# Loading the weights and x in groups between layer-norm transposes, and pacing q attention against the GLU, in a two-layer transformer kernel on one Trainium2 core

## The chip, the cores and the metric

The kernel runs on one core of one Trainium2 chip. A core has a matrix engine (TensorE, PE in the profile), a vector engine (VectorE, DVE), a scalar engine (ScalarE, ACT), a general engine (GpSimd, POOL) and a small engine that mostly issues transfers (SyncE, SP). Each has its own stream of instructions and works through it in order; they wait for each other on semaphores. Transfers between the main memory and the on-chip memory (SBUF) are issued by an instruction of SP or ACT and are then carried out by 16 DMA engines. Matrix products land in PSUM, which has eight banks here.

The metric is the device time of one execution in microseconds (us); lower is better. Three runs of the kernel before took 1256.72, 1257.25 and 1257.52 us, median 1257.25.

## The reference

x has 2048 tokens of width 576. Two kinds of layer alternate, twice each, every one with a layer norm in front and a residual sum behind:

```python
x = x + A(layernorm(x)); x = x + B(layernorm(x))
x = x + A(layernorm(x)); x = x + B(layernorm(x))

# A: linear attention, 32 heads of width 18
q, k, v = split(x @ wqkv)
phi(t)  = concat(softmax(t @ w_phi), softmax(-(t @ w_phi)))   # per head, 18 -> 36
kv = phi(k)^T @ v          # summed over all tokens
z  = sum of phi(k) over all tokens
o  = (phi(q) @ kv) / (phi(q) . z + 1e-6)
A  = o @ wo

# B: gated linear unit, width 4608, no activation function
B  = ((x @ w_gate) * (x @ w_up)) @ w_down
```

All inputs are bf16. kv and z need phi(k) of every token before the first token's q attention can be finished. That is a barrier in each layer.

## The kernel before

**Tiles.** A *state* is 128 tokens; there are 16. A *block* is two states, 256 tokens; there are 8. x stays in SBUF (`x_sb`) from beginning to end. Gate and up weights (`Wg`, `Wu`, `Wr`) stay there as well; the down weight is read again for each block, in 18 chunks of two 128-row tiles each, through a ring of four slots (`wdr`).

**Stages.** In the order of the work:

1. *Loads* (`t_load`, line 619). x, w_phi, the raw q and k weights, Wv, Wo, then Wr, Wg and Wu, 10.6 MB of them in ten loads. All are issued on ACT's queue.
2. *Fusing* (`t_fuse`, line 671, `t_fuse2`, line 696). w_phi is the same for every token, so the kernel multiplies it into the q and k weights once: PE transposes a raw weight (L688), ACT copies it out (`WT`, L691), PE multiplies it with the block-diagonal w_phi (L709), DVE copies the result to `Wk` or `Wq` (L716). The q weights follow when two states of k attention are through.
3. *Layer norm* of one block (`t_ln`, line 725). DVE computes statistics (L734, L739), ACT the reciprocal root (L746 to L750), POOL normalises each state (L755), ACT copies a tail (L760), and SP issues one transposing transfer per state (L764), which brings `xln` into `xT`, with the features on the partitions. Three pairs of `xln` buffers are in turn.
4. *k attention* of one state (`t_ain`, line 873). PE projects (`proj`, L778), `softmax_front` (line 782) computes both softmaxes over ACT, DVE and POOL (max and min on DVE, L793 and L798; differences on POOL, L803, and DVE, L811; exponentials on ACT, L818 and L820; sums on DVE, L825; the division by the sums as a product on POOL, L839). `t_v` (line 842) projects v (L857 is its copy). PE adds phi(k)^T v to PSUM (L867).
5. *Barrier* (`t_barrier`, line 919). The sums over all 16 states are masked into `BD`.
6. *q attention* of one state (`t_aout`, line 948). The same `softmax_front`, then transposes (L964), the product with `BD` (L981), the division (L993 to L1006), a transpose (L1017), the product with Wo (L778 again) and the sum into x (L1030).
7. *GLU* of one block (`t_bmain`, line 1083, `t_down`, line 1122). First the *gate phase*: 648 matmuls of gate and up (L1070), which take six PSUM banks, copied and multiplied into `hT` (L1113, L1115). Then the *down phase*: 36 tiles times two states, each a matmul of 512 columns (L1137) and one of 64 (L1140). `t_bepi` (line 1150) adds the result to x (L1158) and signals `("x2", L, b)`: layer L, block b.

Layer 1 of A runs for all tokens first. The A part of layer 2 up to its barrier is woven into the GLU of layer 1: when a block is through (`after`, line 1215), its layer norm, k attention and `t_kv` are started.

**What sets the order.** The program is written by a planner (`Sched`, line 246). Each piece of work above is a generator, a *thread* with a priority, that yields lists of instructions for an engine, transfers, requests for buffers and PSUM banks, `wait` and `sig`. The planner keeps its own clock: a duration for each instruction, and for each transfer a start on its queue, a speed and a latency (lines 428 to 439). It takes again and again the instruction list that could start first on that clock, with the higher priority first in a tie, and appends it to its engine's stream. `wait` and `sig` only act in the planner, on the order of the streams. On the chip there are just the semaphores that the data need: a reader waits for its writer, a writer for the readers before it. `record_dma` (line 133) does this for transfers: a transfer waits on its issuing engine's stream, and what stands behind it in that stream waits too.

While a gate phase is planned, the GLU thread holds a lock, and no other thread gets a PSUM bank (line 284). So attention's matmuls stand in the down windows between the gate phases. Before a gate phase of block b the GLU thread waits for its policy (`pol1`, line 1238, `pol2`, line 1246): the q attention of block b+1 must be planned, and in layer 1, from b = 2 on, the k attention of layer 2 for block b-2.

`t_q` (line 1178) starts q attention: for each block in turn it waits until `xT` is there and, from the second block on, for the barrier, starts both states, and waits for the second state of the block before. It does not look at the GLU. Here are the lines:

```python
for b in range(NB):
    yield ("wait", ("xT", L, b))
    if b >= s.early // 2:
        yield ("wait", ("BD", L))
    for j in range(2):
        yield ("go", s.t_aout(L, 2 * b + j), ...)
```

The down-weight thread (`t_wd`, line 1038) and the GLU thread are started once all ten gate and up loads are planned (`wloaded`). In the kernel before this is at once, and the first four chunks are issued at the very start.

Of the kernel before, what the change touches and what calls it, by code (L numbers as in the profile page):

```python
# [17 lines left out]
class Tracker:  # L18
    def __init__(self):
        self.ops = {e: [] for e in ENGINES}  # L20
        self.count = {e: 0 for e in ENGINES}
        self.know = {e: {} for e in ENGINES}
        self.snap = {}
        self.fin = {}
        self.lastw = {}
        self.readers = {}
        self.lastacc = {}
        self.dma_groups = []
        self.pend_w = {}
        self.pend_r = {}  # L30
        self.stats = {"ops": 0, "waits": 0, "multiwait": 0, "pe_multiwait": 0}
# [214 lines left out]
class Sched:  # L246
# [74 lines left out]
    def run(self):  # L321
        tr = self.tr
        while True:
            progressed = False
            again = True
            while again:
                again = False
                for th in list(self.threads):
                    while th.req is not None and th.req[0] not in ("ops", "dma", "acq", "acqn"):
                        r = th.req  # L330
# [52 lines left out]
            for th in self.threads:  # L383
                r = th.req
# [21 lines left out]
            r = th.req  # L406
            if r[0] == "ops":
                eng = r[1]
                t = est
                first = True  # L410
                t_beg = t
                for o in r[2]:
                    deps = tr.deps_for(eng, o.reads, o.writes, o.excl, True, o.order)
                    if not first:
                        t = max(t, tr.ready_time(deps))
                    if eng == "pe" and o.mode != self.pe_mode:
                        self.pe_mode = o.mode
                        if not first:
                            t += self.pe_switch
                    first = False  # L420
                    fin = t + o.dur
                    tr.record(eng, o.emit, o.reads, o.writes, o.excl, fin, deps)
                    self.busy[eng] += o.dur
                    t = fin
                if self.log is not None:
                    self.log.append((th.name, eng, t_beg, t, len(r[2]), self.free_at[eng]))
                self.free_at[eng] = t
            else:
                _, group, emit, reads, writes, nbytes, dram_write = r[:7]
                immediate = r[7] if len(r) > 7 else False  # L430
                issue = est
                queue = r[9] if len(r) > 9 else "sp"
                start = max(issue, self.dma_free[queue])
                xfer = nbytes / self.dma_bw
                self.dma_free[queue] = start + xfer
                sp_time = r[8] if len(r) > 8 else 60.0
                fin = max(start + xfer + self.dma_lat, issue + 2.1 * sp_time)
                tr.record_dma(group, emit, reads, writes, fin, queue, dram_write, immediate)
                self.free_at[queue] = issue + sp_time
# [37 lines left out]
class K:  # L477
    def __init__(self, nc, A_x, A_wqkv, A_w_phi, A_wo, B_w_gate, B_w_up, B_w_down, out):
        self.nc = nc
        self.A_x, self.A_wqkv, self.A_w_phi, self.A_wo = A_x, A_wqkv, A_w_phi, A_wo  # L480
        self.wg, self.wu, self.wd, self.out = B_w_gate, B_w_up, B_w_down, out
        self.NPS, self.NSM, self.NVX, self.NET, self.NXP, self.NWD, self.NG, self.NO = 2, 4, 2, 3, 2, 4, 2, 1
        self.early = 2
        self.qlead = 3
        self.bias = {10: 300.0}
        self.tr = Tracker()
        self.sc = Sched(self.tr)
        self.stack = ExitStack()
# [130 lines left out]
    def t_load(self):  # L619
        s, tr = self, self.tr  # L620
        xv = s.A_x[0].rearrange("(t p) d -> p t d", p=128)
        wqkv = s.A_wqkv

        def grp(name, items, ev):
            g = tr.dma_group(name)
            for emit, writes, nbytes in items:
                yield ("dma", g, emit, (), writes, nbytes, False, False, 60.0, "act")
            yield ("dmaclose", g)
            yield ("sig", ev)

        def xload(j):
            return grp("x%d" % j, [((lambda e: e.dma_start(s.x_sb[:, 4 * j:4 * j + 4, :], xv[:, 4 * j:4 * j + 4, :])),
                                    [("x", t, c_) for t in range(4 * j, 4 * j + 4) for c_ in range(2)], 128 * 4 * D * 2)], ("ld", "x", j))
# [8 lines left out]
        items = []  # L642
        for t in range(NT):
            h0 = T0[t] // DH
            items.append(((lambda e, t=t, h0=h0: e.dma_start(s.wst[:, t, :], s.A_w_phi[h0:h0 + HT].rearrange("j d f -> (j d) f"))),
                          [("wst",)], TW * DH * 2))
        yield from grp("wphi", items, ("ld", "wphi"))
        for kt in range(5):
            yield from rawload("k", kt)

        def w5(W, src, key, name):
            return grp(name, [
                ((lambda e: e.dma_start(W[:, 0:4, :], src[0:512].rearrange("(k p) n -> p k n", p=128))), [(key,)], 512 * D * 2),
                ((lambda e: e.dma_start(W[0:64, 4, :], src[512:576])), [(key, 0)], 64 * D * 2)], ("ld", name))

        yield from w5(s.Wv, wqkv[:, 2 * D:3 * D], "Wv", "wv")
        for j in range(1, 4):
            yield from xload(j)
        for kt in range(5):
            yield from rawload("q", kt)  # L660
        yield from w5(s.Wo, s.A_wo, "Wo", "wo")
        wgv = s.wg[0:512, :].rearrange("(k p) n -> p k n", p=128)
        wuv = s.wu[0:512, :].rearrange("(k p) n -> p k n", p=128)
        items = [((lambda e: e.dma_start(s.Wr[0:64, :], s.wg[512:576, :])), [("Wr",)], 64 * FF * 2),
                 ((lambda e: e.dma_start(s.Wr[64:128, :], s.wu[512:576, :])), [("Wr",)], 64 * FF * 2)]
        for k in range(4):
            items.append(((lambda e, k=k: e.dma_start(s.Wg[:, k, :], wgv[:, k, :])), [("Wg",)], 128 * FF * 2))
            items.append(((lambda e, k=k: e.dma_start(s.Wu[:, k, :], wuv[:, k, :])), [("Wu",)], 128 * FF * 2))
        yield from grp("wgu", items, "wloaded")

    def t_fuse(self, which):
        s = self
# [505 lines left out]
    def t_q(self, L):  # L1178
        s = self

        def pair_done(b):
            yield ("wait", ("x1", L, 2 * b))
            yield ("wait", ("x1", L, 2 * b + 1))
            yield ("go", s.t_ln(b, ("xTB", L, b)), 8, "lnB%d_%d" % (L, b))

        yield ("wait", ("ain", L, NS - s.qlead))
        for b in range(NB):
            yield ("wait", ("xT", L, b))
            if b >= s.early // 2:
                yield ("wait", ("BD", L))  # L1190
            for j in range(2):
                yield ("go", s.t_aout(L, 2 * b + j), 7 + (NS - 2 * b - j) / 100.0, "aout%d_%d" % (L, 2 * b + j))
            yield ("go", pair_done(b), 8, "pd%d_%d" % (L, b))
            if b >= 1:
                yield ("wait", ("x1", L, 2 * b - 1))

    def t_layer1(self):
        s = self
        gots = yield ("acqn", ["pb"], 3)
        s.kvb = [g_[1] for g_ in gots]  # L1200
        yield ("wait", "init")
# [109 lines left out]
```

## Time and profile before

| | value |
|---|---|
| median of three runs | 1257.25 us |
| the profiled execution's own time | 1257.18 us |
| its span in the profile | 1255.4 us |
| mean granted TensorE clock | 0.985 of full speed |
| PE busy | 1125.3 us (90%) |
| DVE, ACT, POOL busy | 591.9, 438.0, 272.8 us |
| read from HBM | 100.59 MB |
| transfers of ACT's queue (q10) | 15.66 MB |
| transfers of SP's queue (q1) | 97.81 MB |

The span is the time from the first to the last instruction of the trace; the difference to the execution's time, 1.8 us, lies around it. Busy PE time is modelled, and a matmul that follows close upon another overlaps with it, so a PE that is busy for 100% of a stretch is not one at its peak. The profile's views used below are: the chain of work that ended last (each piece with its start, its length and what it was), the timeline (start, length, engine, line, operation, tiles, count, and the idle time before it with what ended it), the stretches (for each stretch its length, then the busy time and count of PE, PE's weight loads, DVE, ACT and POOL, the granted clock, the share of the DMA engines and GB/s; with a line given, of that line's instructions alone), and the list of transfer issues. L1070 and the like are lines of the kernel.

### The profile page before, as it was taken

To read this page: it belongs to the slowest core of one execution; us is meant where nothing else is said; L and a number is where in the kernel's file an instruction comes from. 1 tells how busy PE (TensorE), PEld (TensorE's weight loads), DVE (VectorE), ACT (ScalarE), POOL (GpSimd) and SP (SyncE) were. 2 spreads that over 40 slices of the span, in tenths; PEclk is the share of its full clock that TensorE was granted. 3 is DMA by queue.
4 is the path that set the end of the run, shared out by engine and by line. 5 is a ranking of instruction groups with operands and counts; after the bars stand their busy time and mean duration, and the time that the engine had idled before them with its cause. 6 is when DMAs were issued, how large, how long until landed. Compare 5 with 4: busy or idle time off the path is not lost.

```text
span 1255.4 us, 33464 instructions
## 1 busy us (share of the span) xinstructions
PE 1125.3 (90%) x15104; PEld 853.9 (68%) x15172; DVE 591.9 (47%) x1243; ACT 438.0 (35%) x976; POOL 272.8 (22%) x271
## 2 busy tenths in 40 slices
PE   1377689999999999999999759999999999999998
PEld 1155477787786867677777448778685858677684
DVE  3188775848653434343434475674832313122131
ACT  2167544536441314141413344554521212121120
POOL 1268731514311011111111342240500000000000
PEclk9989899999999999999999889999999999999999
DMA  9820011514406061515151401240616060523414
GB/s 293 281 38 12 1 22 36 158 13 110 104 14 179 15 168 32 152 31 153 39 144 50 133 1 23 78 126 10 165 41 182 11 180 21 162 69 113 124 59 142
DMA packets 130315, 115.61 MB, mean 92 GB/s; under 512 B 48892, under 2 KB 129020, under 8 KB 129020
## 3 DMA queue, kind: packets, MB, share of 16 engines
q1 hardware_dynamic: 123520, 97.81, 29.3%
q10 hardware_dynamic: 6652, 15.66, 3.6%
q8 instruction: 119, 1.95, 0.6%
q14 instruction: 24, 0.20, 0.0%
HBM read 100.59 MB, written 2.36 MB: 82 GB/s over the span
## 4 chain that ended last, share of the span: by engine, by line
PE 74%; DMA 13%; DVE 5%; ACT 3%; POOL 2%; ACTq 1%; issue 1%; SPq 0%; DVEq 0%
PE ps L1070 45%; PE ps L1137 12%; DMA wdr<-in_B_w_down_dram 11%; PE ps L778 10%; DMA xT<-xln 3%; PE ps L1140 2%; POOL dd L839 2%; PE ps L964 1%; PE ps L981 1%; PE ps L867 1%; PE ps L1017 1%; DVE o L1006 1%; DVE ss L825 1%; DVE mxmn L793 1%; DVE mxmn L798 1%
## 5 line engine op out<-in xcount | busy, mean ns | idle before, releaser
L1070 PE MATMUL ps<-xT,Wg 64*128 64x256 bf16 x4608 | 568.0, 269 | 1.7 <-DMA xT<-xln 1.7
L1070 PE MATMUL ps<-xT,Wu 64*128 64x256 bf16 x4608 | 568.5, 269 | 0.9 <-DVE x_sb L1158 0.7
L1070 PEld LDWEIGHTS ps<-xT,Wg 64*128 64x128 bf16 x4608 | 429.5, 94 | 32.5 <-issue 2.9
L1070 PEld LDWEIGHTS ps<-xT,Wu 64*128 64x128 bf16 x4608 | 431.7, 94 | 28.7 <-DVE x_sb L1158 1.8
L1115 DVE TENSOR_TENSOR hT<-ps,gsb 128x512 bf16<-128x512 f32 x288 | 199.1, 691 | 341.7 <-ACT gsb L1113 341.3
L1113 ACT CAST gsb<-ps 128x512 bf16<-128x512 f32 x288 | 168.5, 585 | 543.9 <-PE ps L1070 543.3
L1137 PE MATMUL ps<-wdr,hT 128*128 128x512 bf16 x1084 | 293.6, 381 | 20.5 <-DMA wdr<-in_B_w_down_dram 19.7
L1140 PE MATMUL ps<-wdr,hT 128*128 128x64 bf16 x1152 | 221.9, 193 | 5.2 <-DMA wdr<-in_B_w_down_dram 1.2
L1137 PEld LDWEIGHTS ps<-wdr,hT 128*128 128x128 bf16 x1152 | 112.5, 98 | 161.3 <-DMA wdr<-in_B_w_down_dram 45.0
L839 POOL TENSOR_TENSOR dd<-dd,ss 128x576 bf16<-128x576 bf16 x128 | 145.7, 1163 | 112.1 <-ACT ss L833 112.1
L1070 PE MATMUL ps<-xT,Wr 64*128 64x256 bf16 x1152 | 167.3, 269 | 0.0
L803 POOL TENSOR_TENSOR dd<-psb,mxmn 128x576 bf16<-128x576 bf16 x64 | 74.2, 1163 | 324.8 <-DVE mxmn L793 324.8
L1140 PEld LDWEIGHTS ps<-wdr,hT 128*128 128x128 bf16 x1152 | 112.9, 98 | 0.9
L755 POOL TENSOR_SCALAR xln<-x_sb,nmean,rstd 128x576 bf16<-128x576 bf16 x64 | 51.9, 821 | 240.1 <-ACT rstd L750 213.9
L1158 DVE TENSOR_TENSOR x_sb<-ps,x_sb 128x512 bf16<-128x512 f32 x32 | 21.9, 685 | 164.3 <-PE ps L1140 164.3
L825 DVE TENSOR_REDUCE ss<-dd 128x64 f32<-128x1152 bf16 x64 | 85.2, 1341 | 19.7 <-ACT dd L820 19.5
L778 PE MATMUL ps<-Wv,xT 128*128 128x378 bf16 (+1 forms) x320 | 54.5, 306 | 26.1 <-issue 17.6
L793 DVE TENSOR_REDUCE mxmn<-psb 128x32 f32<-128x576 bf16 x64 | 47.6, 744 | 54.6 <-ACT psb L790 54.6
L1070 PEld LDWEIGHTS ps<-xT,Wr 64*128 64x128 bf16 x1152 | 65.3, 94 | 6.8
L790 ACT CAST psb<-ps 128x288 bf16<-128x288 f32 x128 | 50.3, 398 | 41.0 <-PE ps L778 38.7
L778 PE MATMUL ps<-Wk,xT 128*128 128x288 bf16 x320 | 50.6, 300 | 9.7 <-DMA xT<-xln 7.0
L778 PEld LDWEIGHTS ps<-Wv,xT 128*128 128x128 bf16 x320 | 29.9, 103 | 39.8 <-issue 25.7
(67 smaller groups left out, 930.7 us busy)
## 6 DMA issues: line engine op xcount, KB each, us to landing
wdr<-in_B_w_down_dram SPq DMA_DIRECT2D x288, 288.0 KB, 3.3
Wg<-in_B_w_gate_dram ACTq DMA_DIRECT2D x4, 1152.0 KB, 22.4
Wu<-in_B_w_up_dram ACTq DMA_DIRECT2D x4, 1152.0 KB, 24.8
x_sb<-in_A_x_dram ACTq DMA_DIRECT2D x4, 576.0 KB, 7.4
out_dram<-x_sb SPq DMA_DIRECT2D x8, 288.0 KB, 2.9
Wraw<-in_A_wqkv_dram ACTq DMA_DIRECT2D x8, 144.0 KB, 6.2
xT<-xln SPq DMA_TRANSPOSE x64, 2.9
Wv<-in_A_wqkv_dram ACTq DMA_DIRECT2D x1, 576.0 KB, 6.0
```

Source lines behind the costliest of these rows:

```text
L755: ops.append(Op(800, (lambda e, j=j: e.tensor_scalar(xln[:, sl[j], 0:576], x_sb[:, ss[j], :], nm[:, sl[j]:sl[j] + 1], rstd[:, sl[j]:sl[j] ...
L778: ops.append(Op(d_pe(n), (lambda e, lhsT=lhsT, rhs=rhs, k=k: e.matmul(s.ps[:, bank, 0:n], lhsT, rhs, start=(k == 0), stop=(k == 4))), read ...
L790: yield ("ops", "act", [Op(d_actc(288), (lambda e, h=h, bank=bank: e.copy(psb[:, pz, 288 * h:288 * h + 288], s.ps[:, bank, 0:288])), reads ...
L793: ops = [Op(680, (lambda e: e.tensor_reduce(mxmn[:, pz, 0, :], p3, AX.X, ALU.max)), reads=[("psb", pz, 0), ("psb", pz, 1)], writes=[("mx", ...
L803: yield ("ops", "pool", [Op(1170, (lambda e: e.tensor_tensor(d1, p3, mxb, ALU.subtract)), reads=[("psb", pz, 0), ("psb", pz, 1), ("mx", pz ...
L825: Op(1320, (lambda e: e.tensor_reduce(ss[:, sm, :].rearrange("p (b g) -> p b g", b=2), e4, AX.X, ALU.add)), reads=s.ddk(sm, 0) + s.ddk(sm, ...
L839: yield ("ops", "pool", [Op(1150, (lambda e, ev=ev, rb=rb: e.tensor_tensor(ev, ev, rb, ALU.mult)), reads=s.ddk(sm, br) + [("ss", sm)], wri ...
L1070: out.append(Op(54.3, (lambda e, bank=bank, cs=cs, lhsT=lhsT, rhs=rhs, st=st, sp=sp: e.matmul(ps[:, bank, cs], lhsT, rhs, start=st, stop=s ...
L1113: yield ("ops", "act", [Op(540, (lambda e, g=g, gb=gb: e.copy(gsb[:, g, :], ps[:, gb, :])), reads=[("gu", gb)], writes=[("gsb", g)], excl= ...
L1115: yield ("ops", "dve", [Op(625, (lambda e, g=g, ub=ub, p=p: e.tensor_tensor(hT[:, p, :], ps[:, ub, :], gsb[:, g, :], ALU.mult)), reads=[(" ...
L1137: ops.append(Op(d_pe(512), (lambda e, lhsT=lhsT, bank=bank, slot=slot, fi=fi, f=f: e.matmul(ps[:, bank, 0:512], lhsT, s.wdr[:, slot, fi, 0 ...
L1140: ops.append(Op(d_pe(64) + 3, (lambda e, lhsT=lhsT, sl=sl, slot=slot, fi=fi, f=f: e.matmul(ps[:, Z, 64 * sl:64 * sl + 64], lhsT, s.wdr[:, ...
```

## The change

Three things change.

*The queue and the order of the loads.* Every load of `t_load` goes to SP's queue instead of ACT's. x is loaded block by block (eight loads) instead of four loads of two blocks. w_phi comes in two loads instead of five. x of block 1 is planned behind the raw k weights, x of block 2 behind Wv. x of block b, from 3 on, is planned when the transposes of block b-3 of the first layer norm are; raw q goes behind x of block 5, Wo behind x of block 6. The ten gate and up loads are planned in groups: three when the transposes of block 5 are planned, three with block 6, four with block 7. `wloaded` comes at the end of them.

*The planner's time for an issue.* A transfer without a time of its own now occupies its queue for 480 ns on the planner's clock instead of 60. That concerns the loads and the down-weight chunks; the transposes keep their 1250.

*The pace of q attention.* In layer 1, block b's q attention, from b = 4 on, is started only when block b-4 is through the GLU; in layer 2, from b = 3 on, when block b-3 is.

```diff
-                sp_time = r[8] if len(r) > 8 else 60.0
+                sp_time = r[8] if len(r) > 8 else 480.0
...
+        self.pace = (4, 3)
...
-                yield ("dma", g, emit, (), writes, nbytes, False, False, 60.0, "act")
+                yield ("dma", g, emit, (), writes, nbytes, False)
...
-        def xload(j):
-            return grp("x%d" % j, [((lambda e: e.dma_start(s.x_sb[:, 4 * j:4 * j + 4, :], xv[:, 4 * j:4 * j + 4, :])),
+        def xload(b):
+            return grp("x%d" % b, [((lambda e: e.dma_start(s.x_sb[:, 2 * b:2 * b + 2, :], xv[:, 2 * b:2 * b + 2, :])),
...
+        items = [((lambda e: e.dma_start(s.wst[:, 0:4, :], s.A_w_phi[0:4 * HT].rearrange("(t j) d f -> (j d) t f", j=HT))), [("wst",)], TW * DH * 8),
+                 ((lambda e: e.dma_start(s.wst[:, 4, :], s.A_w_phi[H - HT:H].rearrange("j d f -> (j d) f"))), [("wst",)], TW * DH * 2)]
         yield from grp("wphi", items, ("ld", "wphi"))
         for kt in range(5):
             yield from rawload("k", kt)
+        yield from xload(1)
...
         yield from w5(s.Wv, wqkv[:, 2 * D:3 * D], "Wv", "wv")
-        for j in range(1, 4):
-            yield from xload(j)
-        for kt in range(5):
-            yield from rawload("q", kt)
-        yield from w5(s.Wo, s.A_wo, "Wo", "wo")
+        yield from xload(2)
+        for b in range(3, NB):
+            yield ("wait", ("xT", 1, b - 3))
+            yield from xload(b)
+            if b == 5:
+                for kt in range(5):
+                    yield from rawload("q", kt)
+            if b == 6:
+                yield from w5(s.Wo, s.A_wo, "Wo", "wo")
...
-        yield from grp("wgu", items, "wloaded")
+        g = tr.dma_group("wgu")
+        for i, (emit, writes, nbytes) in enumerate(items):
+            if i % 3 == 0 and 5 + i // 3 < NB:
+                yield ("wait", ("xT", 1, 5 + i // 3))
+            yield ("dma", g, emit, (), writes, nbytes, False)
+        yield ("dmaclose", g)
+        yield ("sig", "wloaded")
...
             yield ("wait", ("xT", L, b))
+            if b >= s.pace[L - 1]:
+                yield ("wait", ("x2", L, b - s.pace[L - 1]))
...
-            yield ("wait", ("ld", "x", b // 2))
+            yield ("wait", ("ld", "x", b))
```

More of the change, by code (lines that the diff above doesn't have):

```diff
@@ L626, in grp @@
             for emit, writes, nbytes in items:
-                yield ("dma", g, emit, (), writes, nbytes, False, False, 60.0, "act")
+                yield ("dma", g, emit, (), writes, nbytes, False)
             yield ("dmaclose", g)
             yield ("sig", ev)
-        def xload(j):
-            return grp("x%d" % j, [((lambda e: e.dma_start(s.x_sb[:, 4 * j:4 * j + 4, :], xv[:, 4 * j:4 * j + 4, :])),
-                                    [("x", t, c_) for t in range(4 * j, 4 * j + 4) for c_ in range(2)], 128 * 4 * D * 2)], ("ld", "x", j))
+        def xload(b):
+            return grp("x%d" % b, [((lambda e: e.dma_start(s.x_sb[:, 2 * b:2 * b + 2, :], xv[:, 2 * b:2 * b + 2, :])),
+                                    [("x", t, c_) for t in range(2 * b, 2 * b + 2) for c_ in range(2)], 128 * 2 * D * 2)], ("ld", "x", b))
         def rawload(which, kt):
@@ L641, in t_load @@
         yield from xload(0)
[L642 to L646, printed above, removed]
+        items = [((lambda e: e.dma_start(s.wst[:, 0:4, :], s.A_w_phi[0:4 * HT].rearrange("(t j) d f -> (j d) t f", j=HT))), [("wst",)], TW * DH * 8),
+                 ((lambda e: e.dma_start(s.wst[:, 4, :], s.A_w_phi[H - HT:H].rearrange("j d f -> (j d) f"))), [("wst",)], TW * DH * 2)]
         yield from grp("wphi", items, ("ld", "wphi"))
```

## The prediction

> **What bounds the kernel now.** I read first the chain of work that ended last, in order of time, because shares of busy time mix stages with different limits. Three of its pieces frame the stage ahead of the first GLU block (start us, length us, what):
>
> ```profile
> 25.81 26.80 DMA xT<-xln
> 52.75 5.18 PE ps L778 x20
> ...
> 171.23 35.54 PE ps L1070 x648
> ```
>
> Nothing but a layer-norm transpose is on the chain for 26.8 us, and the first gate block starts at 171.23 us. The timeline of the first 66 us tells why (start, length, engine, line, tile, count, idle time before):
>
> ```profile
> 5.74 1.54 DVE L734 BATCH_NORM_STATS2 st<-x_sb 128x6 f32<-128x288 bf16 x4 [4.41 <-DMA x_sb<-in_A_x_dram]
> ...
> 20.15 0.45 ACTq L668 DMA_DIRECT2D Wu<-in_B_w_up_dram  x1
> 20.64 1.29 ACT L691 COPY WT<-ps 126x640 bf16<-126x640 bf16 x2 [6.25 <-issue]
> ...
> 29.97 0.34 DVE L716 CAST Wk<-ps 64x198 bf16<-64x198 f32 x1
> ...
> 66.22 4.52 POOL L839 TENSOR_TENSOR dd<-dd,ss 128x576 bf16<-128x576 bf16 x4 [3.10 <-ACT ss L833]
> ```
>
> x is there at 5.7 us, but ACT issues loads until 20.6 us and only then takes up the fusing of Wk (L691) and its part of the layer norm. Then the transposes stand beside the bulk loads. Their size and speed: the page's list of DMA issues (KB each, us to landing) and the stretch from 20 to 40 us (last columns: DMA share 1.03, 342 GB/s):
>
> ```profile
> Wg<-in_B_w_gate_dram ACTq DMA_DIRECT2D x4, 1152.0 KB, 22.4
> wdr<-in_B_w_down_dram SPq DMA_DIRECT2D x288, 288.0 KB, 3.3
> 20.00:40.00 20.00, 4.69 (x40) 4.06 (x40) 9.20 (x30) 5.14 (x16) 3.23 (x4) 1.00 1.03 342
> ```
>
> From 66 us on, POOL carries the k attention: two states need 8.5 us (116.86 to 125.39), of which it idles 1.76:
>
> ```profile
> 116.86 4.52 POOL L839 TENSOR_TENSOR dd<-dd,ss 128x576 bf16<-128x576 bf16 x4 [1.76 <-ACT ss L833]
> 121.34 2.29 POOL L803 TENSOR_TENSOR dd<-psb,mxmn 128x576 bf16<-128x576 bf16 x2
> 125.39 4.52 POOL L839 TENSOR_TENSOR dd<-dd,ss 128x576 bf16<-128x576 bf16 x4 [1.76 <-ACT ss L833]
> ```
>
> Behind 171 us PE is the bound. Between two gate phases lies a down phase; only there can attention get PSUM banks (the gate thread holds the lock). I asked for the stretches of these down windows. Layer 1, windows behind blocks 0, 1 and 3, with the sum over windows 0 to 4; then layer 2, windows 0, 1, 5 and the sum over 0 to 5:
>
> ```profile
> 206.77:249.86 43.09, 42.15 (x420) 29.66 (x427) 35.66 (x96) 26.30 (x59) 20.63 (x20) 1.00 0.49 134
> 284.31:329.07 44.76, 43.73 (x429) 30.81 (x437) 36.99 (x95) 25.73 (x61) 21.42 (x20) 1.00 0.51 133
> ...
> 430.20:455.91 25.71, 24.40 (x202) 13.93 (x208) 10.26 (x18) 7.19 (x17) 6.89 (x6) 1.00 0.61 178
> ...
> sum 171.98, PE 163.84 PEld 105.92 DVE 107.85 ACT 76.47 POOL 64.29; mean PE 32.77 PEld 21.18 DVE 21.57 ACT 15.29 POOL 12.86
> ```
>
> ```profile
> 793.96:837.04 43.08, 42.12 (x421) 29.71 (x427) 35.67 (x96) 26.30 (x59) 20.63 (x20) 1.00 0.51 134
> 871.49:911.57 40.08, 39.64 (x389) 27.65 (x398) 32.88 (x93) 23.54 (x55) 18.50 (x18) 1.00 0.54 141
> ...
> 1119.20:1139.73 20.53, 18.50 (x143) 8.95 (x147) 1.40 (x3) 0.58 (x1) 0.00 (x0) 1.00 0.77 223
> sum 169.33, PE 157.61 PEld 94.11 DVE 76.70 ACT 53.01 POOL 40.76; mean PE 26.27 PEld 15.69 DVE 12.78 ACT 8.84 POOL 6.79
> ```
>
> How many states of q attention each holds comes from line 981 alone, ten matmuls a state:
>
> ```profile
> 206.77:249.86 43.09, 5.15 (x60) 4.25 (x60) 1.00 0.49 134
> 284.31:329.07 44.76, 4.01 (x50) 3.42 (x50) 1.00 0.51 133
> 793.96:837.04 43.08, 5.14 (x60) 4.25 (x60) 1.00 0.51 134
> 871.49:911.57 40.08, 5.16 (x60) 4.12 (x60) 1.00 0.54 141
> ```
>
> So the twelve states of blocks 2 to 7 lie in the first two windows (the twelfth of layer 1 in the third), and the later windows are bare. A bare one isn't full. On the chain its down matmuls run at this pace:
>
> ```profile
> 683.00 0.22 PE ps L1137
> 683.21 0.03 PE ps L1140
> 683.24 0.22 PE ps L1137
> ```
>
> A pair of matmuls starts every 0.24 to 0.25 us (683.00 to 683.24); 72 pairs at 0.245 are 17.6 us; the bare window has 20.53, so about 2.9 us are waits. The ring of four wdr slots explains them: a slot comes back after 0.98 us of use and a landing of 3.3 us, and four of them at 4.3 us give 1.07 us a chunk against 0.98 of matmuls, with hand-over on top.
>
> **The change part by part.** The sums are made against the profiled execution, 1257.18 us with a span of 1255.4, 0.07 us under the median of the runs.
>
> *Start.* All early loads go from ACT's queue to SP's. ACT then no longer has the issues up to 20.15 us before its work. The raw k weights are the third group on SP, eighth issue at the latest; at half a microsecond an issue (the row at 20.15) they are out by 5 us, and with the 4 to 5 us that x needed to land at the start (5.74) they are there by about 9: an estimate from these two rows. From the first WT copy to the last Wk cast it took 20.64 to 30.31, 9.7 us; so Wk is ready near 19 us instead of 30. The layer norm runs beside it: x of the first block alone at about 5 us, statistics 1.5, two POOL passes, and the transposes go out near 10 us. What stands ahead of them on SP's queue is x0, w_phi, five raw k, x1, Wv and x2, about 2.2 MB, 6.5 us at 342 GB/s, gone by about 10 us. With 3.3 us to landing, as wdr has, they are there near 13 us, ahead of Wk. So the k projections start at 19 instead of 54 us.
>
> From there to the first L839 pass the old trace has 12 us (the projections begin at 52.75 on the chain with those of Wv, a microsecond and a half before those of Wk; L839 is at 66.22). That puts L839 near 31.5 instead of 66.2: 34.7 us. Against that, POOL then has more layer norms left:
>
> ```profile
> 0.00:66.20 66.20, 8.11 (x10) 1.00 0.92 278
> ```
>
> This is line 755 alone, two passes a block: five blocks were through by 66.2 us, while the new kernel will have three or four. One more pair is 1.62 us (8.11 / 5). I take **-33 us**; ends -37 (no extra layer norm, Wk two us sooner) and -20 (next paragraphs).
>
> *The bulk loads on SP.* The waits in the load list are the planner's: they fix where a load stands among SP's instructions, and SP then waits for the layer norm of the transpose ahead. Queued behind such a waiting transpose are later x tiles (x of block b behind the transposes of block b-3, so two blocks are in hand), raw q, Wo and the ten gate and up loads. These are let out behind the transposes of blocks 5, 6 and 7, three, three and four. If they follow the first L839 at 31.5 us in steps of some 10 us (8.5 for two states and 1.6 for a layer norm), that is at about 40, 50 and 62 us. The last four, 4.7 MB, take 13.8 us at 342 GB/s: all there before 85 us, and the gate needs them at about 138. The cover is some 50 us; without it each microsecond late would be one of the whole.
>
> The price is on the transposes. In the row above, a transpose beside 10 MB on the other queue needed 26.8 us. Behind the loads in its own queue it waits at most for the three loads ahead, 3.5 MB, 10.3 us; with it the transposes of block 6 land by 63 us and those of block 7 by 75. States 12 to 15, which need them, come to L839 six and seven steps of 9 us behind the first, at 86 and 95 us, and are projected some 13 us sooner, at 73 and 82. So I cost it at nothing, with 12 us as the far end. [...] The mechanism is the second rival below.
>
> *q attention held back, layer 2.* Blocks 3 to 7 now start when blocks 0 to 4 of the GLU are done, and each must be through before the gate phase behind its window (pol2). So windows 0 to 5 hold one pair of states each. On the path lies the larger of PE's work and the pair's own chain. PE: a state costs (40.08 - 17.6) / 6 = 3.75 us in window 1, 4.25 in window 0, so a window is 17.6 + 7.5 = 25.1 if the pair fills the waits for wdr, and 20.5 + 8.5 = 29.0 if it fills none. The pair's chain, from a nearly empty stretch before the second layer's gate, where block 1 goes through from its projections to its last output projection:
>
> ```profile
> 732.14 2.56 PE ps L778 x15
> ...
> 753.20 0.63 PE ps L778 x5
> ```
>
> 21.7 us, which fits beneath 25.1. I take the middle, 26.9, and 26 for window 0, some of whose work is done before the gate: 26 + 5 x 26.9 = 160.5 against 169.33, **-8.8 us**; ends -18.7 (six at 25.1) and +4.7 (six at 29.0).
>
> *Layer 1.* Blocks 4 to 7 wait for blocks 0 to 3, which leaves each two windows. Window 0 holds four states: 17.6 + 4 x 3.75 to 4.25, about 33. Windows 1 to 4 hold a k pair and a q pair: the k window without q has 25.71, less its 2.9 of waits 22.8, plus 7.5 is 30.3 at the least, and 25.71 + 8.5 = 34.2 at the most; I take 33.3, nearer the upper end because two chains share the window. 33 + 4 x 33.3 = 166.2 against 171.98, **-5.8 us**; ends -18 and -1.
>
> The raised 480 ns per issue in the planner (line 436) changes orders only; I cost it at nothing, a microsecond either way. Sum: 1257.2 - 33 - 8.8 - 5.8 = 1209.6, forecast **1209**.
>
> **The rivals.** *Pacing gives nothing* (the waits for wdr stay, the windows only trade places): 1257.2 - 33 = 1224. For it: PE's sums are the same, and the planner's landing time is 3.05 us where the trace has 3.3. Against: window 1 of layer 2 has six states at 3.75 us with hardly any wait. 22%.
>
> *Transposes queue behind weights.* If states 12 to 15 do wait, or the x tiles come late behind SP's waits, 12 us of the start's gain are lost: 1221. [...] 12%.
>
> *Slower.* The held-back pair follows the down matmuls instead of lying between them, because PE takes its instructions in the planned order. Then a window is 20.5 + 21.7 = 42.2 in layer 2 (five of them, 237 with window 0) and 25.7 + 21.7 = 47.4 in layer 1 (four, 223 with window 0): +68 and +51, with the start 1343; with half of the chain uncovered, halfway between 1343 and 1209, 1276. It decides from 5.3 us per window over the forecast (47.6 / 9): 32 us in layer 2, 38.6 in layer 1. Against it: in windows 0 and 1 the pairs do lie between the down matmuls. 3%.
>
> *It doesn't do what it says*: the planner's clock lets the waits pass where the chip's would not, and the first softmax is hardly earlier. About 1257. 3%.
>
> *All fills*: both pacing terms near their low ends and the start at -37: about 1188. 8%.
>
> **How the numbers follow.** That leaves 52% for the forecast. A measurement of this kernel can tell about 0.2% from no change. The range from 1191 to 1232 holds the forecast with its ends, the first two rivals with a few us of slack, and part of the last. Faster by over 0.2%: all but the slower case and the half of the case without effect: 0.95; same 0.02; slower 0.03.
>
> **What would show it.** The first L839 near 31 us; no DMA piece of over 10 us on the chain ahead of the gate; the first gate phase at 138 us (133 to 150). Line 981 with twenty matmuls in each of layer 2's windows 0 to 5, and those windows at 25 to 29 us. In layer 1 forty in window 0 and twenty in windows 1 to 4, at 30 to 35. The step from layer 1 to layer 2 as long as it is. Wrong it would be if the gate waits for Wg, if SP's transposes keep POOL waiting, or if PE idles at the ends of windows for L1006 or L839.

## The result, and the profile after

The changed kernel takes 1215.47 us, median of 4 runs (1214.19 to 1218.63); the kernel before took 1256.99 us beside it (1255.17 to 1257.52, 4 runs). The ratio is 0.9676, with a 95% interval from 0.9655 to 0.9697: 41.5 us less. The profiled execution took 1214.19 us, its span is 1212.5, 42.9 us shorter than that of the kernel before. Behind the edit, lines are up to 11 higher: L839 is L848 now, L981 is L990, L1070 is L1079.

One thing in the section on the kernel before is wrong: the layer norm has two pairs of `xln` buffers, not three. No number of the prediction hangs on it.

First the chain of waits of the changed kernel, the pieces that answer to those shown of before:

```profile
9.84 2.82 DMA xT<-xln
12.85 1.68 PE ps L787 x5
...
140.70 35.54 PE ps L1079 x648
```

The first transpose is on the chain for 2.8 us instead of 26.8, and it goes out at 9.8 us. The first gate phase starts 30.5 us sooner (171.23 before). The timeline of POOL, the first product of k attention, and the setting of BD, which ends the barrier:

```profile
26.43 4.52 POOL L848 TENSOR_TENSOR dd<-dd,ss 128x576 bf16<-128x576 bf16 x4 [3.09 <-ACT ss L842]
...
113.72 0.35 POOL L950 MEMSET BD<- 54x133 bf16 x2
```

In the kernel before these two stand at

```profile
66.22 4.52 POOL L839 TENSOR_TENSOR dd<-dd,ss 128x576 bf16<-128x576 bf16 x4 [3.10 <-ACT ss L833]
...
145.05 0.35 POOL L941 MEMSET BD<- 54x133 bf16 x2
```

So k attention begins 39.8 us sooner, but its barrier comes only 31.3 us sooner. Some 8.5 us of the start's gain are given back inside the stage. DVE's timeline shows where:

```profile
55.12 1.53 DVE L743 BATCH_NORM_STATS2 st<-x_sb 128x6 f32<-128x288 bf16 x4
...
79.89 0.27 DVE L748 BATCH_NORM_AGGREGATE mv<-st 128x2 f32<-128x12 f32 x2
...
91.66 0.75 DVE L802 TENSOR_REDUCE mxmn<-psb 128x32 f32<-128x576 bf16 x1 [9.01 <-ACT psb L799]
```

The statistics of block 7 are through at 56.7 us, but their short second step comes 23 us later. The transposes of that block go out at 84.4, and DVE idles 9.0 us, from 82.6 on, until the first of the states that need them has been projected. In the hole the granted clock is lower as well. From 85 to 91 us it is 0.50, and the first four groups of projections behind the hole take 4.6 us (87.0 to 91.7); the next four, of the same shapes, take 2.6 us at a granted clock of 1.00 (91.7 to 94.3). So some 2 us of DVE's wait are slower matmuls, by an estimate from these two times.

The down windows, layer 1 (windows 0 and 1, and the sum over 0 to 4, 171.98 before), then layer 2 (windows 0, 1 and 5, and the sum over 0 to 5, 169.33 before):

```profile
176.24:208.60 32.36, 31.56 (x303) 20.91 (x308) 20.45 (x59) 14.95 (x33) 10.12 (x10) 1.00 0.55 151
244.07:276.73 32.66, 31.95 (x292) 21.04 (x298) 22.96 (x52) 16.00 (x39) 15.27 (x14) 1.00 0.51 143
...
sum 162.99, PE 159.34 PEld 105.03 DVE 112.28 ACT 78.96 POOL 71.19; mean PE 31.87 PEld 21.01 DVE 22.46 ACT 15.79 POOL 14.24
```

```profile
756.13:783.66 27.53, 23.98 (x212) 13.95 (x218) 7.96 (x25) 5.28 (x11) 1.63 (x2) 1.00 0.66 181
819.14:846.56 27.42, 26.00 (x232) 15.97 (x238) 14.91 (x37) 10.49 (x23) 8.49 (x8) 1.00 0.61 173
...
1069.23:1096.28 27.05, 26.09 (x231) 16.00 (x238) 14.91 (x37) 10.20 (x23) 8.48 (x8) 1.00 0.60 170
sum 162.76, PE 154.06 PEld 93.86 DVE 82.49 ACT 56.85 POOL 44.02; mean PE 25.68 PEld 15.64 DVE 13.75 ACT 9.48 POOL 7.34
```

The two long windows of each layer are gone, and the short ones behind them hold a pair each: windows 0 to 5 of layer 2 are all alike, and so are windows 0 to 4 of layer 1. Line 990 alone, ten matmuls a state of q attention, in the same four rows:

```profile
176.24:208.60 32.36, 3.40 (x40) 2.84 (x40) 1.00 0.55 151
244.07:276.73 32.66, 1.54 (x20) 1.26 (x20) 1.00 0.51 143
...
756.13:783.66 27.53, 1.70 (x20) 1.26 (x20) 1.00 0.66 181
819.14:846.56 27.42, 1.86 (x20) 1.25 (x20) 1.00 0.61 173
```

Window 0 of layer 1 holds four states, every other window of these eleven holds one pair. Not all of the windows' gain reaches the end. Before, 21 matmuls of the next gate phase stood inside a crowded window, and that phase was a microsecond shorter on the chain:

```profile
249.86 34.45 PE ps L1070 x627
```

There were three such phases; now each has its full 648 matmuls and 35.5 us. So the spans divide like this: start -30.5 us (gate 0 to gate 0); layer 1 from its first gate phase to the end of its last -7.4 (506.1 to 498.7); the step between the layers +0.1; layer 2 from its first gate phase to the end -5.1 (497.0 to 491.9). The sum is -42.9.

### The profile page after: what moved, and what is told of

Its sections match the earlier page's. It is cut to its first block, busy times and chain, and to the rows that moved or that the text cites. A ratio compares the mean times of both kernels' runs of the same rounds, so it can differ in the third digit from the quotient of the medians.

```text
span 1212.5 us, 33465 instructions
## 1 busy us (share of the span) xinstructions
PE 1124.0 (93%) x15096; PEld 857.0 (71%) x15172; DVE 597.6 (49%) x1243; ACT 442.7 (37%) x976; POOL 273.3 (23%) x271
## 4 chain that ended last, share of the span: by engine, by line
PE 78%; DMA 10%; DVE 5%; POOL 3%; ACT 2%; issue 1%; SPq 0%; DVEq 0%; POOLq 0%
PE ps L1079 47%; PE ps L1146 12%; PE ps L787 11%; DMA wdr<-in_B_w_down_dram 9%; PE ps L1149 3%; POOL dd L848 2%; PE ps L973 1%; DVE ss L834 1%; PE ps L990 1%; PE ps L876 1%; DVE o L1015 1%; DMA xT<-xln 1%; PE ps L1026 1%; POOL xln L764 1%; DVE mxmn L807 1%
## 5 line engine op out<-in xcount | busy, mean ns | idle before, releaser
L1079 PE MATMUL ps<-xT,Wg 64*128 64x256 bf16 x4608 | 568.7, 269 | 1.7 <-DMA xT<-xln 1.7
L1079 PE MATMUL ps<-xT,Wu 64*128 64x256 bf16 x4608 | 568.6, 269 | 0.0
L1079 PEld LDWEIGHTS ps<-xT,Wg 64*128 64x128 bf16 x4608 | 431.9, 94 | 32.5 <-issue 3.3
L1079 PEld LDWEIGHTS ps<-xT,Wu 64*128 64x128 bf16 x4608 | 431.9, 94 | 27.3
L1146 PEld LDWEIGHTS ps<-wdr,hT 128*128 128x128 bf16 x1152 | 112.6, 98 | 145.5 <-DMA wdr<-in_B_w_down_dram 31.7
L848 POOL TENSOR_TENSOR dd<-dd,ss 128x576 bf16<-128x576 bf16 x128 | 145.6, 1165 | 104.9 <-ACT ss L842 104.9
L1079 PE MATMUL ps<-xT,Wr 64*128 64x256 bf16 x1152 | 156.9, 269 | 0.0
L799 ACT CAST psb<-ps 128x288 bf16<-128x288 f32 x128 | 50.3, 397 | 43.9 <-PE ps L787 41.5
L1079 PEld LDWEIGHTS ps<-xT,Wr 64*128 64x128 bf16 x1152 | 56.1, 94 | 6.8
L827 ACT ACTIVATE dd<-dd 128x576 bf16<-128x576 bf16 x64 | 43.4, 678 | 43.8 <-DVE dd L820 43.6
```

What stands on the lines that cost most here:

```text
L799: yield ("ops", "act", [Op(d_actc(288), (lambda e, h=h, bank=bank: e.copy(psb[:, pz, 288 * h:288 * h + 288], s.ps[:, bank, 0:288])), reads ...
L848: yield ("ops", "pool", [Op(1150, (lambda e, ev=ev, rb=rb: e.tensor_tensor(ev, ev, rb, ALU.mult)), reads=s.ddk(sm, br) + [("ss", sm)], wri ...
L1079: out.append(Op(54.3, (lambda e, bank=bank, cs=cs, lhsT=lhsT, rhs=rhs, st=st, sp=sp: e.matmul(ps[:, bank, cs], lhsT, rhs, start=st, stop=s ...
L1146: ops.append(Op(d_pe(512), (lambda e, lhsT=lhsT, bank=bank, slot=slot, fi=fi, f=f: e.matmul(ps[:, bank, 0:512], lhsT, s.wdr[:, slot, fi, 0 ...
```

## The experiments

Two theories stood against each other for each part. For the start: what counts is *when* the loads go out, or *that ACT has none* to issue. For the windows: the pacing fills the waits for `wdr`, or something else in the edit (the planner's 480 ns) moved them. A third question was where the 8.5 us of the start went. Every ratio is to the kernel before, run beside it on the same chip; the kernel before had 1259.6, 1260.7 and 1261.4 us in the three groups of runs below.

**The two parts alone.** e1 takes the pacing out of the changed kernel; e2 puts it alone into the kernel before.

```diff
-        self.pace = (4, 3)
+        self.pace = (8, 8)          # e1: on the changed kernel
```

```diff
+        self.pace = (4, 3)          # e2: on the kernel before
...
+            if b >= s.pace[L - 1]:
+                yield ("wait", ("x2", L, b - s.pace[L - 1]))
```

> The changed kernel without the pacing of q attention (it starts as soon as its data allow, as before). If start and pacing are two parts that add, the start keeps its gain (first gate phase at 140.7 us, as in the changed kernel) and the two GLU layers fall back by what they gained between the two traces, 7.4 us in layer 1 and 5.1 us in layer 2: about 1228 us, with twelve states of q attention in the first two windows of each layer again. Rival: the windows gained from the planner's 480 ns per issue, not from the pacing: then 1215 us.

> The kernel before with the pacing of q attention alone; loads, their queue and the planner's 60 ns stay as before. If the parts add: 12.5 us less than the kernel before, about 1244.5 us, the first gate phase still at 171 us, windows of layer 1 near 32.6 and of layer 2 near 27. Rival (the windows gained from the 480 ns, or pacing pays only together with the new start): 1257 us.

e1: 1229.85 us, ratio 0.9760 (0.9741 to 0.9778). e2: 1248.49 us, ratio 0.9917 (0.9904 to 0.9930). The loads are worth 2.4%, the pacing 0.8%, and the product of the two, 0.968, is the ratio of the whole. In e1 the first two windows of layer 1 are back at 43.4 and 44.8 us; in e2 the first gate phase starts at 172.3 us and the windows of layer 1 are 32.6 to 32.9. The two parts add, and the pacing does the work in the windows. What it fills there are the waits for `wdr`: the weight loads of the down matmuls sat idle for it for 45.0 us in the kernel before, for 34.0 in e2 and for 31.7 in the changed kernel.

**The planner's time for an issue.** e4 is the changed kernel with 60 ns again.

```diff
-                sp_time = r[8] if len(r) > 8 else 480.0
+                sp_time = r[8] if len(r) > 8 else 60.0
```

> The changed kernel with 60 ns per issue on the planner's clock instead of 480. Theory: it only moves orders, 1213 to 1218 us, the same as the changed kernel. Rival: the planner then puts loads and chunks where SP can't yet issue them, and the windows or the start lose more than 3 us.

1214.13 us, ratio 0.9643 (0.9621 to 0.9665). The changed kernel itself had 0.9676 in its first runs and 0.9671 (0.9657 to 0.9685) in the next group. The intervals overlap; the 480 ns are worth nothing that these runs can tell.

**When, or on which queue.** e6 issues the same groups at the same planned places from ACT; e7 leaves the old order and issues it all from SP.

```diff
-                yield ("dma", g, emit, (), writes, nbytes, False)
+                yield ("dma", g, emit, (), writes, nbytes, False, False, 480.0, "act")   # e6, both places
```

```diff
-                yield ("dma", g, emit, (), writes, nbytes, False, False, 60.0, "act")
+                yield ("dma", g, emit, (), writes, nbytes, False)                        # e7, kernel before
```

> The changed kernel once more, unaltered, as a base for the three runs beside it on the same chip: 0.9676 of the kernel before, within 0.002.

> The changed kernel with its loads in the same groups and at the same planned places, but issued on ACT's queue (480 ns each on the planner's clock) instead of SP's. If the gain of the start comes from when the loads go out, not from which queue carries them, it keeps nearly all: first gate phase between 138 and 147 us, total within 6 us of the changed kernel (ACT pays some half a microsecond for each of 35 issues, 17 us spread over a stage in which it isn't the bound). Rival: what matters is that ACT has nothing to issue, and that loads stand behind the transposes in one queue; then the first L848 comes some 10 us or more later and the gate at 150 us or later.

> The kernel before with its loads in the old order and all at once, but on SP's queue; nothing else changed. ACT is then free from the start, and Wk is ready by about 15 us. If transposes that stand behind loads in one queue wait for them, the first transposes, behind 15.66 MB at 342 GB/s, land at about 50 us, the first L839 comes at 55 to 66 us, and the total lies within 10 us of the kernel before (1247 to 1260 us). Rival: freeing ACT alone is what gained; then the first L839 comes at about 27 us and the total is about 1230 us.

The changed kernel once more: 1219.6 us, ratio 0.9671. e6: 1223.07 us, ratio 0.9704 (0.9686 to 0.9721), 3.5 us behind it, its first gate phase at 145.4 us against 142.1. e6 keeps x in single blocks and w_phi in two loads too; what these are worth apart from the order was not tried. e7: 1263.30 us, ratio 1.0029 (1.0017 to 1.0042): all of the start's gain is gone, although ACT had nothing to issue. The first four chunks of down weights, which the kernel before issues at the very start, stand behind the loads here. The timeline of SP, the chain, and a stretch of e7:

```profile
19.04 0.43 SPq L668 DMA_DIRECT2D Wu<-in_B_w_up_dram  x1
19.51 22.77 SPq L1045 DMA_DIRECT2D wdr<-in_B_w_down_dram  x4
42.32 143.30 SPq L764 DMA_TRANSPOSE xT<-xln  x20
```

```profile
42.32 11.52 DMA xT<-xln
53.89 4.17 PE ps L778 x15
```

```profile
20.00:42.00 22.00, 0.00 (x0) 0.00 (x0) 0.00 (x0) 0.00 (x0) 0.00 (x0) 1.00 1.01 352
```

POOL had its first layer norms by 12 us. Then SP needs 22.8 us for the issue of four chunks (3.8 to 6.9 us each), with the DMA engines at a share of 1.01, and the transposes wait behind them, first in SP's stream and then 11.5 us in the queue: the last chunk landed at 53.2 us, the first transpose at 53.8. For 22 us not one engine computes. The first L839 comes at 65.5 us, as in the kernel before (66.2). It is the order in time that pays; the queue is worth some 3 us.

**The layer norm of block 7.** e3 raises the priority of all layer norms of the first stage, e9 that of the last alone.

```diff
-            yield ("go", s.t_ln(b, ("xT", 1, b)), 6, "lnA1_%d" % b)
+            yield ("go", s.t_ln(b, ("xT", 1, b)), 6.5, "lnA1_%d" % b)                            # e3
+            yield ("go", s.t_ln(b, ("xT", 1, b)), 6.5 if b == NB - 1 else 6, "lnA1_%d" % b)      # e9
```

> The changed kernel with priority 6.5 instead of 6 for the layer norms of the first stage, so that they go ahead of k attention in a tie. In the changed kernel the first L848 came 39.8 us sooner but the barrier only 31.3 us sooner, and the layer norm of block 7 stands behind twelve states of k attention (82.4 us) with idle engines after it. Theory: the planner starves that layer norm because VectorE is always taken by threads of higher priority; with the priority raised the hole of 6 to 9 us behind it goes, the first gate phase comes at about 133 us, and the time is 1207 to 1210 us. Rival 1: the loads ahead of the transposes in SP's queue hold the last blocks up; SP's stream is unchanged here, so 1215 us. Rival 2: POOL and VectorE are the bound of the stage and the work only trades places: 1213 to 1217 us.

> The changed kernel with priority 6.5 only for the layer norm of block 7. Raising it for all blocks took the hole away (the barrier came 3.7 us sooner) but the first L848 came 5 us later, as POOL did layer norms ahead of it, and two states ran in step, 8.5 us a pair with POOL idle 1.76, where the changed kernel had 3.6 us a state. Theory: the hole and the early order are two things; with the last norm alone moved, the first L848 stays at 26.4 us, the hole goes, the gate comes at 131 to 135 us and the total is 6 to 9 us below the changed kernel. Rival: any layer norm put between the states puts them in step again, and the gate stays at 137 us or later.

e3: 1213.30 us, ratio 0.9639 (0.9622 to 0.9657), first gate phase at 137.8 us: less than expected. The time is the one that rival 2 named, and it can't be told from e4's in the same group (1214.13). Its POOL timeline shows why. Six of the eight layer norms lie ahead of the first product and the other two right behind it, the first product comes 5 us later, and then two states run in step with a fixed idle time:

```profile
31.26 4.52 POOL L848 TENSOR_TENSOR dd<-dd,ss 128x576 bf16<-128x576 bf16 x4
...
73.25 4.53 POOL L848 TENSOR_TENSOR dd<-dd,ss 128x576 bf16<-128x576 bf16 x4 [1.76 <-ACT ss L842]
```

e9: 1213.64 us, ratio 0.9620 (0.9603 to 0.9638), against 0.9671 for the changed kernel in the same group, 6 us. Its first gate phase starts at 133.5 us, 8.7 sooner. POOL's timeline of e9, first product, last layer norm, and barrier:

```profile
26.74 4.52 POOL L848 TENSOR_TENSOR dd<-dd,ss 128x576 bf16<-128x576 bf16 x4 [3.09 <-ACT ss L842]
...
59.06 1.62 POOL L764 TENSOR_SCALAR xln<-x_sb,nmean,rstd 128x576 bf16<-128x576 bf16 x2
...
106.74 0.35 POOL L950 MEMSET BD<- 54x133 bf16 x2
```

The hole is gone: the second step of block 7's statistics starts at 56.4 us, as soon as they are through, and from there to the barrier DVE never idles more than 1.7 us at a time. From the first product to the barrier e9 needs 80.0 us; the changed kernel needs 87.3, the kernel before 78.8. In the planner, a ready instruction of DVE starts when DVE is free; where several could start at that moment, priority decides. k attention has priorities from 6.01 up, the layer norm 6. As long as DVE was always taken, the layer norm of block 7 lost each tie. The rival of e9 was half right: its states do run in step behind the layer norm, but this did not hold the gate at 137 us. The states' faster pace in the changed kernel was to a part only the work left out. Stretches of L848 alone, first the changed kernel, then e9:

```profile
0.00:82.40 82.40, 29.58 (x26) 0.94 0.63 162
82.40:114.00 31.60, 11.50 (x11) 0.64 0.55 198
```

```profile
0.00:83.10 83.10, 27.18 (x24) 0.94 0.73 201
83.10:107.00 23.90, 12.44 (x11) 0.84 0.32 121
```

At nearly the same time the one has 26 passes and no layer norm of block 7, the other 24 passes and that layer norm with its transposes long done. In the second rows, up to the barrier, eleven passes take 31.6 us at a granted clock of 0.64 in the one and 23.9 us at 0.84 in the other. e9 shows what moving that one layer norm is worth; that ties on DVE and nothing else held it back is read from the planner's rule and the idle gap, and e3 and e9 agree with it.

**Forcing the slower rival.** e10 sets the pace of layer 2 to 2, so that a pair can start only when the gate phase in front of it waits for it.

```diff
-        self.pace = (4, 3)
+        self.pace = (4, 2)
```

> The changed kernel with pace (4, 2): in layer 2 the q attention of block b waits for block b-2 of the GLU, and the gate phase of block b-1 waits for it, so nothing is left to lie beside it. This makes the slower rival of the prediction happen on purpose. Theory: a pair's chain, 21.7 us, then stands behind each of the six down phases of 20.5 us (windows of about 42 us instead of 27): some 90 us more than the changed kernel, about 1305 us. Rival: PE's own work is what counts, wherever the pair stands: within 10 us of the changed kernel.

1308.22 us, ratio 1.0377 (1.0355 to 1.0399). Two of its windows (stretches), and inside the first of them, on the chain, the first and the last projections of the pair:

```profile
840.77:882.50 41.73, 29.89 (x233) 17.69 (x238) 14.12 (x33) 9.66 (x19) 6.85 (x6) 0.88 0.47 135
917.98:960.29 42.31, 30.53 (x233) 18.01 (x238) 14.18 (x33) 9.66 (x19) 6.85 (x6) 0.88 0.46 133
```

```profile
861.14 1.85 PE ps L787 x15
...
881.10 1.40 PE ps L787 x10
```

From 861.14 to 882.50 are 21.4 us; the windows last 41 to 44 us, where the prediction had 42.2 for this case. So the change is one step away from a loss of 47 us against the kernel before: pace 3 leaves just one gate phase of slack, pace 2 none.

**Five wdr slots.** e11 gives the ring one more slot; four small layer-norm tiles share one allocation so that it fits.

```diff
-        self.NPS, self.NSM, self.NVX, self.NET, self.NXP, self.NWD, self.NG, self.NO = 2, 4, 2, 3, 2, 4, 2, 1
+        self.NPS, self.NSM, self.NVX, self.NET, self.NXP, self.NWD, self.NG, self.NO = 2, 4, 2, 3, 2, 5, 2, 1
...
+        self.sml = A("sml", [128, 6 * self.NXP + 1], F32)
+        self.epst = self.sml[:, 6 * self.NXP:6 * self.NXP + 1]
...
-        self.lnv = A("lnv", [128, 2 * self.NXP], F32)
+        self.lnv = self.sml[:, 0 * self.NXP:2 * self.NXP]
```

> The changed kernel with five wdr slots instead of four (four small layer-norm tiles share one allocation to make room). If the waits of a bare down window come from the ring (a slot returns after some 4.3 us, four give a chunk each 1.07 us, five each 0.86, against 0.98 of matmuls), bare windows shrink from 20.6 to 17.6 to 18.5 us, windows with a pair of q states from 27 to 25 or 26, and the total falls by 15 to 25 us, to about 1197. Rival: the waits are bandwidth or landing times that grow with what is in flight: less than 5 us.

1200.97 us, ratio 0.9523 (0.9501 to 0.9546). A window with a pair and a bare one of e11:

```profile
1058.15:1084.49 26.34, 25.91 (x232) 15.99 (x238) 14.89 (x37) 10.29 (x22) 8.41 (x8) 1.00 0.60 171
1119.97:1138.31 18.34, 17.81 (x143) 9.04 (x148) 1.43 (x3) 0.58 (x1) 0.00 (x0) 1.00 0.82 248
```

The bare window falls from 20.6 to 18.3 us, so most of its 2.9 us of waits came from the ring. The window with a pair falls only from 27.1 to 26.3: the pair had filled all but 0.7 us. By the ratios, 0.9671 and 0.9523, e11 is some 19 us faster than the changed kernel. Between the two profiled spans lie 16.1 us: some 9 in the windows without q attention and in the step between the layers (81.2 to 79.1 us), some 7 in the eleven windows with q attention. The weight loads of the down matmuls now sit idle for `wdr` for 7.3 us in all, after 31.7.

**Another pace.** e13 sets (4, 4): two pairs in window 0 of layer 2, windows 5 and 6 bare.

```diff
-        self.pace = (4, 3)
+        self.pace = (4, 4)
```

> The changed kernel with pace (4, 4): layer 2 then holds two pairs in window 0 and one in windows 1 to 4, and windows 5 and 6 are bare. If each window with a pair fills its waits for wdr, one more bare window and one with two pairs cost or gain 1 to 3 us: within 0.3% of the changed kernel. Rival: window 0, which holds the back half of one pair only, is the badly filled one (27.5 us for less work than the 27 of the others), and a second pair there gains 4 us or more.

1216.69 us, ratio 0.9653 (0.9630 to 0.9676), no different from the changed kernel. Window 0 takes 32.7 us, windows 1 to 4 about 27, window 5 21.1. Together these six take 161.7 us, against 162.8 in the changed kernel: what window 0 gains by a second pair is nearly what window 5 loses by standing bare.

**Together.** e12 is e11 with the change of e9 (the two diffs above in one kernel).

> Five wdr slots and the raised priority of the last layer norm together. They act in different stages, so the gains should add: what the ring of five gives, and 6 us more (ratio to the kernel before lower by 0.005 than that of the ring of five).

1192.56 us, ratio 0.9461 (0.9440 to 0.9482): 0.0062 below e11, about as far as e9 alone is below the changed kernel (0.0051). This version beats both kernels, the one before by 5.4%, the changed one by some 2.2%.

## Why the prediction held, and where its terms were off

The forecast was 1209 us in a range from 1191 to 1232; measured are 1215.5. The mechanism and the sign of each part were right. The sizes:

*Start, -33 forecast, -30.5 measured.* Two errors of opposite sign. The first product was forecast for 31.5 us and came at 26.4. The first raw k weight landed after 2.85 us, not 4 to 5, at 5.2 us instead of 9, and the last cast of Wk ended at 15.1 us, not 19. Then the forecast allowed POOL one layer norm more, 1.6 us, for the rest of the stage. That one was there, four behind the first product instead of three, but the stage gave back 8.5 us up to the barrier and 9.3 up to the gate, since the normalising of block 7 came 26 us after its statistics. The step that failed is "If they follow the first L839 at 31.5 us in steps of some 10 us": the layer norms of blocks 5 and 6 did (44.2 and 56.7 us), that of block 7 did not (82.4). I had counted the planner's waits and not its priorities; e9 has the 8.7 us at the gate, and its stage is 1.2 us longer than that of the kernel before, near the 1.6 forecast.

*Transposes behind the loads.* Costed at nothing, and the chain shows nothing of it. SP's timeline of the changed kernel, the last load of the first group, the transposes of block 6, and those of block 7:

```profile
51.12 0.58 SPq L670 DMA_DIRECT2D Wg<-in_B_w_gate_dram  x1
58.71 3.53 SPq L773 DMA_TRANSPOSE xT<-xln  x2
...
84.41 2.53 SPq L773 DMA_TRANSPOSE xT<-xln  x2
```

That load took 11.0 us to land, to 62.1, so the transposes of block 6 had the last of it before them in the queue; they needed 4.1 and 3.7 us and landed at 62.8 and 63.7. Those of block 7 had nothing before them and needed 2.6 to 2.7. The last gate and up loads went out at 88.6 us, and the gate came at 140.7. In e9 the transposes of block 6 went out 3.3 us behind the same load and needed 7.6 and 7.1 us; it landed at 62.0, they at 62.5 and 63.3. The prediction counted on a transpose waiting for the loads ahead of it in its own queue, which no row of before shows; in these two runs and in e7 the first transpose landed 0.5 to 0.7 us behind the transfer ahead of it.

*Layer 2, -8.8 forecast.* The windows gave -6.6 (162.76 against 169.33), and the gate phase that got its matmuls back took 1.0 of this. Windows 1 to 5 came out as forecast, 26.7 to 27.4 for 26.9 (the middle of the two bounds is 27.05, which is also their mean). Window 0 was the term that was too small: 27.5 for 26, with 23.98 us of PE work, so the ring's waits are only poorly filled there. And the sum set the window alone against the old one, though the old trace has 21 matmuls of the next gate phase inside window 0; they had to come back.

*Layer 1, -5.8 forecast.* The windows gave -9.0 (162.99 against 171.98), less 2.0 for two gate phases. A window of a k pair and a q pair took 32.6 us, not 33.3: two chains in a window filled the waits better than I thought, and did not get into each other's way.

*The rivals.* "Pacing gives nothing" is refuted by e2, whose interval ends at 0.9930. "Transposes queue behind weights" took place for block 6, by a microsecond or so each, and cost nothing that the chain shows; e7 shows the kernel in which it costs the whole gain of the start. "All fills" did not come: the windows of layer 2 stay near 27 us, not 25.1. "Slower" had the right mechanism and the right price, 42 us a window, and did not occur at pace 3; e10 shows it at pace 2. "It doesn't do what it says" fell with the first product at 26.4 us. What the forecast got for the right reason is the place of both gains. That its total is only 6.5 us off owes something to luck: the start's two errors, -5.1 and +7.6, leave +2.5.

## What to carry to other kernels

A bulk load that isn't needed soon costs what it delays: issue it behind the small transfers that the next stage waits for, and judge it by the work that stands still, not by the bandwidth it uses. Work that is held back to fill stalls elsewhere pays as long as it has somewhere to lie; measure its chain once, compare it with the space between its earliest start and the first thing that waits for it, and keep one step of slack. Where a planner writes the order, look for a short step that loses every tie: its price shows up where the stage ends, long after the place where it was passed over.

## What the runs showed of the hardware

*Some issues take long.* In e7, SP issued some thirty loads at about half a microsecond each and then needed 22.8 us for four chunks of 288 KB, with the DMA engines at a share of 1.01. ACT issued as many loads in the kernel before, and its longest issue took 1.75 us. The number of transfers alone does not decide it: in e9, SP issued seven loads of 1152 KB between 65.5 and 69.4 us and then needed 10.4 us for the four chunks. What does limit it was not tried.

*The clock in the windows of e10.* The granted clock was 0.88 in the two windows shown, and 1.00 in those of the changed kernel. In the first of the two, PE has no matmul for 8.0 us (863.6 to 871.6), the granted clock is 0.50 from 869 to 877 us, and 233 matmuls have 29.9 us of PE time, where a window of the changed kernel has 26.0 for 232 (819.14 to 846.56). In the changed kernel's hole the clock fell to 0.50 with no stretch without matmuls longer than 2.2 us (83.0 to 85.2), as far as the trace has them all. What sets the clock was not tried. Work that is held back until it stands alone costs twice here: the chain, and slower matmuls behind the gap.
